# Gradient of w_k by block products after the loop, and the last output pair by block products too

## The chip, the cores and the metric

The kernel runs on one core of one Trainium2 chip. TensorE (PE) multiplies matrices into PSUM; VectorE (DVE) and ScalarE (ACT) do the elementwise work and read PSUM; GpSimd (POOL) and SyncE (SP) issue most of the DMA transfers, each in its own order. The metric is the device time of one execution in microseconds; the lower the better. The time before is the median of three runs, 796.74 us.

## What is computed

The reference is a transformer block, forward and backward, with S = 2048 rows, D = 640 and F = 1728: layernorm, linear attention with 32 heads of 20 columns, output projection, residual, second layernorm, SwiGLU feed-forward (g = silu(x w_gate), u = x w_up, out = (g u) w_down), residual.

```python
x = A_x
h = x + _A_ref(_layernorm(x, axis=-1), A_wqkv, A_wo)
h2 = h + _B_ref(_layernorm(h, axis=-1), B_w_gate, B_w_up, B_w_down)
return h2
```

Outputs are h2 and, for a given grad_out, the gradients of x, w_qkv (640 x 1920: columns of q, k and v), w_o, w_gate, w_up and w_down, all in bfloat16. Two of these matter here. The **gradient of w_k** is xnᵀ · dk, a 640 x 640 result summed over 2048 rows: xn is the normalised input (S x D), dk the gradient at k. The **output** h2 is h1 + m · w_down, where m = g u is S x 1728 and h1 the residual after attention.

## The kernel before, in words

Rows come in ST = 16 tiles of 128 (`P`), columns of D in two halves of 320 (`NCH`), since one PSUM bank takes them singly. PSUM is a pool of four buffers of two banks each (`mm`), handed out in turn. Large SBUF tiles come from pools, also in turn: `big` (five buffers, tag B), `strips` (four buffers, tag S), and two work pools (`wk`). A new tile of a pool waits until the last reader of the buffer's former tile is done.

The work around the change is the end of the kernel. **The dxn loop** (t from 0 to ST + LAG - 1 = 18): for t < 16 it forms dk of row tile t (`ps_dk`, ten matmuls of 320 columns; VectorE finishes dk), and SP issues a DMA transpose of it into `ring`. Three turns later (u = t - LAG) it forms dxn of row tile u (`ps_dxn`, 30 matmuls: dq, pk and dk, all transposed in `ring`, against weights). `load_pqT` brings the transposes of pk and dq three turns ahead; dq itself lies in two strips buffers, `dq[0]` and `dq[1]`, and the transpose of its row tile 15 is the last reader of `dq[1]`. `ln_bwd` then takes dxn through the layernorm's backward: ACT `lb_dy` (L144), DVE reduction (L146) and `lb_k` (L149), ACT `lb_a` (L150), two DVE additions (L151, L152), and a POOL store.

**The gradient of w_k** (`dwqk(1, i)`, i = 0 to 4, L986) takes per 128 rows of the result 2 x 16 matmuls of 320 columns. Tiles 0 to 2 stand in turns 16, 17 and 18 of the loop, ahead of dxn of row tiles 13, 14 and 15; tiles 3 and 4 are filled in behind it in pieces (`dwqk_steps`), between the gradients of w_o (`dwo`) and the first output pair.

**The output stage**: `load_mT` brings m transposed, one DMA transpose per row tile on SP's queue (L1028), four row tiles to a strips buffer; the first five are issued in the loop, the rest later. Row tiles go in pairs. A pair is a 2 x 2 block product with seven products of blocks instead of eight (Winograd's form of Strassen's method): `osum` makes the sums S1 to S4 of the blocks of m on VectorE, T1 to T5 are sums of blocks of w_down made once, and `step_a` to `step_f` (`c22` among them) are the products and the combinations; each pair has 50 matmuls of 320 columns. `NP` = 7 pairs go so; the loop over p runs the first half of pair p between the second half of pair p - 1. Row tiles 14 and 15 are multiplied directly (`tail`, L1266), the last in column chunks of 320, 192 and 128 (`CH15`). `dwv` (gradient of w_v) and `dwo` are filled in once per turn from `small_q`.

Within `tc.manual_schedule` the named engines run in the order in which the code is written; the others are ordered by a scheduler. SP and the DVE are so named around all of this, PE and ACT in the output stage.

Of the kernel before, what the change touches and what calls it, by code (L numbers as in the profile page):

```python
# [15 lines left out]
P = 128  # L16
# [4 lines left out]
def kernel(  # L21
# [901 lines left out]
    with tc.manual_schedule(engines={EngineType.SP, EngineType.DVE}):  # L923
# [71 lines left out]
        def dwqk(which, i, between=None):  # L995
            for n, _ in enumerate(dwqk_steps(which, i)):
                if between and n == 1:
                    between()
# [26 lines left out]
        def load_mT(t):  # L1025
            if t % 4 == 0:
                mTs[t // 4] = strips.tile([P, 4, FT, P], BF16, name="mT", tag="S")
            nc.sync.dma_start_transpose(out=mTs[t // 4][:, t % 4], in_=scr_m[t * P:(t + 1) * P, :])  # L1028

        for t in range(ST + LAG):  # L1030
            if t in (2, 3):
                dwqk(0, t + 1)
# [26 lines left out]
            u = t - LAG  # L1059
            if u < 0:  # L1060
                continue
            if t >= ST:
                dwqk(1, t - ST)
            pkT, dqT, dkT = ring[:, 4 + u % 3], ring[:, 7 + u % 3], ring[:, u % 4]
            ps = mm("ps_dxn")
            for ci, (n0, n1) in enumerate(NCH):
# [3 lines left out]
                                         start=(k == 0 and i == 0), stop=(k == 2 and i == DT - 1))  # L1070
            if u + 3 < ST:
                load_pqT(u + 3)
            if ST - MTA <= u:
                load_mT(u - ST + MTA)
            dx = wk("dx")
            ln_bwd(ps, xn_r[:, u, :], rstd1[:, u:u + 1], dh1[:, u, :], dx[:], 0)
            nc.gpsimd.dma_start(out=o1_v[:, u, :], in_=dx[:])
# [20 lines left out]
            h1rs[t] = wk("h1r", pool=t % 2)  # L1098
            nc.gpsimd.dma_start(out=h1rs[t][:], in_=scr_h1_v[:, t, :])

        NP = ST // 2 - 1
        HK = 6
        ot = big.tile([P, ST * D], BF16, name="ot", tag="B")
        os = big.tile([P, ST * D], BF16, name="os", tag="B")
        B11, B12 = wd[:, 0:HK, 0:320], wd[:, 0:HK, 320:D]
        B21, B22 = wd[:, HK:2 * HK, 0:320], wd[:, HK:2 * HK, 320:D]
        T1, T2, T3, T4 = (ot[:, i * HK * 320:(i + 1) * HK * 320].rearrange("p (k n) -> p k n", k=HK) for i in range(4))
        T5 = ot[:, 4 * HK * 320:4 * HK * 320 + D].rearrange("p (k n) -> p k n", k=2)
        f1 = ot[:, 4 * HK * 320 + D:].bitcast(FP32)
        s1h, u3h = f1[:, 0:320], f1[:, 320:D]  # L1110
        f2 = os[:, 8 * HK * P:].bitcast(FP32)
        u2h = [f2[:, 0:320], f2[:, 320:D]]

        def os_v(p, i):
            o = (4 * (p % 2) + i) * HK * P
# [2 lines left out]
        def mblk(p, r, k):  # L1118
            t = 2 * p + r
            return mTs[t // 4][:, t % 4, k * HK:(k + 1) * HK, :]  # L1120

        def tt(out, in0, in1, op=ALU.subtract):
            nc.vector.tensor_tensor(out=out, in0=in0, in1=in1, op=op)

        def osum(p, i):

# [5 lines left out]

        pa = {}
        pcc = None
        small_q = [(dwo, HG - 1)] + [(dwv, i) for i in range(DT)]

        def prod(out, lhs, rhs, start, stop):
            for k in range(HK):
                nc.tensor.matmul(out, lhsT=lhs[:, k, :], rhs=rhs[:, k, :], start=(start and k == 0),  # L1139
                                 stop=(stop and k == HK - 1), skip_group_check=not start)  # L1140

        def left(out, t, rhs, h, which=(0, 1)):

# [10 lines left out]
        def bank(p):  # L1154
            return pa[p][:, 0, :320], pa[p][:, 1, :320], pcc[:, p % 2, :320]

        def step_a(p):
            pa[p] = mm("ps_oa")
            A, Dk, _ = bank(p)
            prod(A, mblk(p, 0, 0), B11, True, True)  # L1160
            prod(Dk, mblk(p, 0, 1), B21, True, True)
            left(Dk, 2 * p, BL[0], 0)
            tt(s1h, A, h1v(2 * p, 0), ALU.add)
            tt(h1v(2 * p, 0), Dk, s1h, ALU.add)

        def step_b(p):
            prod(bank(p)[2], os_v(p, 0), T1, True, True)

        def step_c(p):
            A = bank(p)[0]  # L1170
            prod(A, os_v(p, 1), T2, False, True)
            tt(u2h[p % 2], A, h1v(2 * p, 1), ALU.add)

        def step_d(p):
            A = bank(p)[0]
            left(A, 2 * p + 1, BL[1], 1, which=(1, 0))
            prod(A, os_v(p, 2), T3, False, True)
            tt(u3h, A, h1v(2 * p + 1, 1), ALU.add)

        def c22(p):  # L1180
# [4 lines left out]

        def step_e(p):
            A = bank(p)[0]
            prod(A, mblk(p, 1, 1), T4, False, True)
            left(A, 2 * p + 1, T5, 0)
            tt(h1v(2 * p + 1, 0), A, h1v(2 * p + 1, 0), ALU.add)  # L1190
            o_store(2 * p + 1)
            pa.pop(p)

        def step_f(p):
            C = pcc[:, p % 2, :320]
            left(C, 2 * p, BL[1], 1, which=(1, 0))
            prod(C, os_v(p, 3), B22, False, True)
            tt(h1v(2 * p, 1), C, u2h[p % 2], ALU.add)
            o_store(2 * p)

        CH15 = [(0, 320), (320, 512), (512, 640)]

        with tc.manual_schedule(engines={EngineType.PE, EngineType.Activation}):
            for t in range(4):
                load_h1(t)
            for t in (5, 6):
                load_mT(t)
            for j in range(2):
                tr_cols(Y[:, j, :], scr_Yt, OH[j])
            tt(T1, B12, B11)  # L1210
            osum(0, 0)
            tt(T2, B22, T1)
            osum(0, 1)
            tt(T3, B22, B12)
            osum(0, 2)
            fill = dwqk_steps(1, 3)
            for j in range(4):
                next(fill)
                dwo(j)
            fill = dwqk_steps(1, 4)  # L1220
            next(fill)
            dwo(4)
            pcc = mm("ps_oc")

            for p in range(NP):
                v = p - 1
                load_h1(2 * p + 4) if 2 * p + 4 < ST else None
                load_h1(2 * p + 5) if 2 * p + 5 < ST else None
                for t in (2 * p + 7, 2 * p + 8):
                    if t < ST:  # L1230
                        load_mT(t)
                for j in range(2 * p + 2, min(2 * p + 4, HG)):
                    tr_cols(Y[:, j, :], scr_Yt, OH[j])
                step_a(p)
                if v < 0:
                    tt(T4, B21, T2)
                    next(fill)
                    step_b(p)
                    step_c(p)
                    osum(p + 1, 0)  # L1240
                    osum(p + 1, 1)
                    next(fill)
                    next(fill)
                    tt(T5, BL[0], BL[1])
                    for k, i in ((0, 3), (1, 2), (1, 3)):
                        osum(p + k, i)
                    continue
                step_d(v)
                step_b(p)
                c22(v)  # L1250
                osum(p + 1, 0)
                step_c(p)
                step_e(v)
                osum(p + 1, 2)
                step_f(v)
                osum(p + 1, 1)
                osum(p + 1, 3)
                if p != 2:
                    f, i = small_q.pop(0)
                    f(i)  # L1260

            pso = {}

            def tail(u, n0, n1, out):
                for j in range(FT - 1):
                    nc.tensor.matmul(out, lhsT=mTs[u // 4][:, u % 4, j, :], rhs=wd[:, j, n0:n1],  # L1266
                                     start=(u == ST - 2 and j == 0), stop=(u == ST - 1 and j == FT - 2))

            v = NP - 1
            p14 = mm("ps_o")  # L1270
            tail(ST - 2, 0, 320, p14[:, 0, :320])
            for f, i in small_q:
                f(i)
            step_d(v)
            tail(ST - 2, 320, D, p14[:, 1, :320])
            c22(v)
            step_e(v)
            step_f(v)
            p15 = [mm("ps_o") for _ in range(2)]
            o15 = [p15[ci % 2][:, ci // 2, :n1 - n0] for ci, (n0, n1) in enumerate(CH15)]  # L1280
            parts = [(ST - 2, n0, n1, p14[:, ci, :320]) for ci, (n0, n1) in enumerate(NCH)]
            parts += [(ST - 1, n0, n1, o15[ci]) for ci, (n0, n1) in enumerate(CH15)]
            for n, (u, n0, n1, out) in enumerate(parts):
                r = slice(64 * (n % 2), 64 * (n % 2) + 64)
                nc.tensor.matmul(out, lhsT=mTs[u // 4][r, u % 4, FT - 1, :], rhs=wd[r, FT - 1, n0:n1],
                                 start=(u == ST - 1), stop=(u == ST - 2))
            tt(half(h1rs[ST - 2][:]), row(p14), half(h1rs[ST - 2][:]), ALU.add)
            o_store(ST - 2)
            h1r = h1rs.pop(ST - 1)
            for ci, (n0, n1) in enumerate(CH15):  # L1290
                tail(ST - 1, n0, n1, o15[ci])
                tt(h1r[:, n0:n1], o15[ci], h1r[:, n0:n1], ALU.add)
                (nc.sync, nc.scalar, nc.sync)[ci].dma_start(out=o0_v[:, ST - 1, n0:n1], in_=h1r[:, n0:n1])


# [28 lines left out]
```

## Time and profile before

| what | before |
|---|---|
| median of the three runs | 796.74 us (796.57 to 804.1) |
| profiled execution: its own time | 796.25 us |
| its span, first to last instruction | 794.5 us |
| PE busy | 790.2 us, 99% of the span |
| DVE busy | 566.9 us, 71% |
| ACT busy | 288.1 us, 36% |
| POOL busy | 172.7 us, 22% |
| DMA moved | 160.11 MB, mean 202 GB/s |
| granted PE clock | 1.000 (mean of the span) |

The profile's own time is 1.75 us above the span, and 0.49 us below the median. Times of single instructions below count from the start of the span. A matmul is pipelined: its busy time, 299 ns for 320 columns, overlaps the next one's, so the rate is read from starts of runs of matmuls: 30 of them in 4.08 us. "Busy" on PE is therefore no measure of distance from the peak.

### The profile page before, as it was taken

The page shows a single profiled execution, that of the slowest core. Times are in us where ns is not written, and L with a number is a line of the kernel's source. Part 1 is how long each engine was busy: PE and PEld are TensorE (multiplying, and loading weights), DVE is VectorE, ACT ScalarE, POOL GpSimd, SP SyncE. Part 2 cuts the span into 40 slices and gives each one's busy share as a digit, 9 for nine tenths or more (in the row PEclk, how much of TensorE's full clock was granted, in tenths as well). Part 3 has the DMA queues.
Part 4 walks back from the last instruction along what each step waited for, and adds up shares of the span by engine and source line. Part 5 has one row for each costly group of instructions (what it writes and reads, how often), then busy time and mean ns, then how long its engine had stood idle before and what let it go on. Part 6 is the DMA issues. An engine that isn't in the chain of part 4 may idle for free.

```text
span 794.5 us, 13629 instructions
## 1 busy us (share of the span) xinstructions
PE 790.2 (99%) x5315; PEld 506.5 (64%) x5315; DVE 566.9 (71%) x1015; ACT 288.1 (36%) x414; POOL 172.7 (22%) x305
## 2 busy tenths in 40 slices
PE   9999999999999999999999999999999999999998
PEld 7776566555555555555666777777777777777665
DVE  7989988894497648845975259998897366635773
ACT  6962532760283045402831123223313133324010
POOL 4600047411201110012042102111221121113230
PEclk9999999999999999999999999999999999999999
DMA  9799999999679877892798657976598959999992
GB/s 259 161 241 305 198 225 254 257 264 234 176 160 236 211 175 191 217 246 68 147 216 217 247 152 193 211 197 168 127 238 177 177 135 155 189 223 261 208 259 83
DMA packets 286705, 160.11 MB, mean 202 GB/s; under 512 B 241564, under 2 KB 275485, under 8 KB 286640
## 3 DMA queue, kind: packets, MB, share of 16 engines
q1 hardware_dynamic: 268912, 99.56, 61.7%
q0 software_dynamic: 14832, 54.36, 22.4%
q10 hardware_dynamic: 2896, 5.33, 2.0%
q8 instruction: 41, 0.67, 0.4%
q14 instruction: 24, 0.20, 0.1%
HBM read 47.68 MB, written 53.66 MB: 128 GB/s over the span
## 4 chain that ended last, share of the span: by engine, by line
PE 97%; DMA 1%; DVE 1%; POOL 0%; issue 0%; SPq 0%; DVEq 0%
PE ps_dhn L108 15%; PE ps_dw L806 10%; PE ps_dxn L1069 8%; PE pu L736 7%; PE ps_wa L646 7%; PE pg L731 7%; PE ps_dwqk L986 5%; PE ps_dm L417 5%; PE ps_kq L305 4%; PE ps_oa L1139 4%; PE ps_wc L646 3%; PE ps_gt L861 3%; PE ps_dp L108 3%; PE ps_dk L108 3%; PE ps_y L508 3%; PE ps_a L571 3%
## 5 line engine op out<-in xcount | busy, mean ns | idle before, releaser
L108 PE MATMUL ps_dhn<-wgT,cols 128*128 128x320 bf16 x864 | 119.5, 299 | 0.0
L108 PEld LDWEIGHTS <-cols 128*128 128x128 bf16 x864 | 84.5, 98 | 32.9
L146 DVE CUSTOM_DVE_ANT_0 lb_a<-lb_dy,hn 128x640 bf16<-128x640 bf16 x32 | 26.4, 825 | 59.0 <-ACT lb_dy L144 59.0
L736 PE MATMUL pu<-wgu,hnT 128*128 128x448 bf16 (+1 forms) x320 | 63.6, 346 | 0.0
L731 PE MATMUL pg<-wgu,hnT 128*128 128x448 bf16 (+1 forms) x320 | 63.6, 346 | 0.0
L806 PE MATMUL ps_dw<-m_s,dh 128*128 128x448 bf16 (+1 forms) x320 | 60.4, 346 | 0.0
L1069 PEld LDWEIGHTS <-ring 128*128 128x128 bf16 x480 | 47.0, 98 | 18.2
L1069 PE MATMUL ps_dxn<-wqkvT,ring 128*128 128x320 bf16 x320 | 51.3, 299 | 0.0
L736 PEld LDWEIGHTS <-hnT 128*128 128x128 bf16 x320 | 31.3, 98 | 27.1
L806 PEld LDWEIGHTS <-dh 128*128 128x128 bf16 x320 | 31.3, 98 | 27.1
L731 PEld LDWEIGHTS <-hnT 128*128 128x128 bf16 x320 | 31.3, 98 | 27.0
L417 PEld LDWEIGHTS <-dh2T 128*128 128x128 bf16 x320 | 31.0, 98 | 25.1
L417 PE MATMUL ps_dm<-wdT,dh2T 128*128 128x448 bf16 (+1 forms) x240 | 46.5, 344 | 0.0
L144 ACT ACTIVATE lb_dy<-ps_dhn,rstd 128x640 bf16<-128x640 f32 x16 | 12.7, 794 | 91.5 <-PE ps_dhn L108 91.5
L305 PE MATMUL ps_kq<-wqk,xnT 128*128 128x320 bf16 x320 | 44.9, 299 | 0.3 <-DMA wqk<-in_A_wqkv_dram 0.2
L752 ACT ACTIVATE dd<-pg 128x896 bf16<-128x896 f32 (+1 forms) x32 | 28.5, 891 | 40.4 <-PE pg L731 38.0
L642 DVE TENSOR_TENSOR dd<-dd 128x3584 bf16<-128x3584 bf16 (+1 forms) x12 | 23.1, 1954 | 22.8 <-PE ps_wa L646 15.6
L305 PEld LDWEIGHTS <-xnT 128*128 128x128 bf16 x320 | 30.9, 98 | 12.7 <-issue 0.5
L646 PEld LDWEIGHTS <-S 128*128 128x128 bf16 x256 | 25.1, 98 | 21.7
L772 POOL DMA_DIRECT2D scr_m<-m_s x16 | 12.1, 758 | 122.6 <-DVE m_s L764 122.6
L986 PEld LDWEIGHTS <-hn 128*128 128x128 bf16 x320 | 31.0, 98 | 12.0
L150 ACT ACTIVATE lb_a<-hn,lb_k 128x640 bf16<-128x640 bf16 x32 | 29.5, 920 | 21.8 <-DVE lb_k L149 18.8
(210 smaller groups left out, 1527.1 us busy)
## 6 DMA issues: line engine op xcount, KB each, us to landing
scr_dT<-stg SPq DMA_DIRECT2D x48, 224.0 KB, 2.6
cols<-scr_dT POOLq DMA_DIRECT2D x6, 1728.0 KB, 8.4
scr_m<-m_s POOLq DMA_DIRECT2D x12, 448.0 KB, 4.6
cols<-scr_dT ACTq DMA_DIRECT2D x2, 1728.0 KB, 10.5
scr_dT<-stg SPq DMA_DIRECT2D x16, 192.0 KB, 2.3
scr_pq<-pqa SPq DMA_DIRECT2D x4, 640.0 KB, 4.6
scr_xnT<-xnT SPq DMA_DIRECT2D x4, 640.0 KB, 5.3
scr_pk<-pk SPq DMA_DIRECT2D x4, 640.0 KB, 4.6
```

Source lines behind the costliest of these rows:

```text
L108: nc.tensor.matmul(ps[:, ci, :320], lhsT=lhs(k), rhs=rhs(k, *NCH[ci]), start=(start and k == 0), stop=(stop and k == n - 1))
L150: nc.scalar.activation(out=a[:], in_=xhat, func=ACT.Identity, scale=k[:, 1:2], bias=k[:, 0:1])
L305: nc.tensor.matmul(ps[:, ci, :320], lhsT=xnT[:, t, k, :], rhs=wqk[:, k, w0 + n0:w0 + n1], start=(k == 0), stop=(k == DT - 1))
L417: nc.tensor.matmul(ps[:, c, :w], lhsT=dh2T[:, kt, (t + c) * P:(t + c + 1) * P], rhs=wdT[:, kt, o:o + w], start=(kt == 0), stop=(kt == DT - 1))
L646: nc.tensor.matmul(out, lhsT=lhs[:, t, :], rhs=rhs[:, t, :], start=(first and t == 0), stop=(t == 7), skip_group_check=not first)
L731: nc.tensor.matmul(pg[:, c, :w], lhsT=hnT[:, kt, (t + c) * P:(t + c + 1) * P], rhs=wg[:, kt, 0:w], start=(kt == 0), stop=(kt == DT - 1))
L736: nc.tensor.matmul(pu[:, c, :w], lhsT=hnT[:, kt, (t + c) * P:(t + c + 1) * P], rhs=wg[:, kt, w:2 * w], start=(kt == 0), stop=(kt == DT - 1))
L752: sig = nc.scalar.activation(out=dg, in_=pg[:, :, :w], func=ACT.Sigmoid)
L806: nc.tensor.matmul(ps[:, c, :w], lhsT=lhs(t), rhs=rhs(t), start=(t == 0), stop=(t == ST - 1))
L986: nc.tensor.matmul(ps[:, ci, :320], lhsT=xn_r[:, t, i * P:(i + 1) * P], rhs=dq[t // 8][:, t % 8, n0:n1] if which == 0 else dk[:, t, n0:n1] ...
L1069: nc.tensor.matmul(ps[:, ci, :320], lhsT=lhs[:, i, :], rhs=rhs[:, i, n0:n1], start=(k == 0 and i == 0), stop=(k == 2 and i == DT - 1))
L1139: nc.tensor.matmul(out, lhsT=lhs[:, k, :], rhs=rhs[:, k, :], start=(start and k == 0), stop=(stop and k == HK - 1), skip_group_check=not s ...
```

## The change

The gradient of w_k leaves the loop. Its result has five row tiles of 128. Tiles 0 to 3 are now taken as two pairs of tiles, with the sum over 2048 rows cut in two halves (`k` = 0, 1, eight row tiles each) and the columns in two halves: again a 2 x 2 block product by seven products, here of 8 matmuls for each of the two tiles (`u`) of a block: 112 matmuls. VectorE makes the sums: `ksum` S1 and S3 of blocks of xn (128 x 1024 each) in turns 16 to 18 of the loop, S2 and S4 later; X1 to X4 (128 x 2560 each) of blocks of dk after the loop. Tile 4 is multiplied directly at the very end, in column chunks of 320, 192 and 128 (`k_tile`), among the last steps of the last output pair. The eighth output pair goes by block products like the others, so `tail` is gone. The sums need room: `sk`, a new strips tile (also for two kept partial results), is allocated in turn 16; `ot` (T1, T2, T4, T5) moves to a strips buffer; T3 is written over B12; `dt` (X1 to X4) takes a big buffer. The m transposes start one turn later.

In the built program, sk has the buffer that dq[1] had, and its first writer, `ksum(1, 0)`, waits for the DMA transposes of dq row tiles 13, 14 and 15. On VectorE it stands right ahead of `ln_bwd` of row tile 13, and X1 right behind `ln_bwd` of row tile 15.

```diff
+        def sk_v(i, u):
+            o = (2 * (i // 2) + u) * 8 * P
+            return sk[:, o:o + 8 * P].rearrange("p (k c) -> p k c", c=P)
+        def ksum(i, u):
+            if i == 1:
+                tt(sk_v(1, u), xb(1, 0, u), xb(1, 1, u), ALU.add)
+            else:
+                tt(sk_v(3, u), xb(0, 0, u), xb(1, 0, u))
...
-            if t >= ST:
-                dwqk(1, t - ST)
+            if t == ST:
+                sk = strips.tile([P, 7 * 8 * P], BF16, name="sk", tag="S")
+                ksum(1, 0)
+            if t == ST + 1:
+                ksum(3, 0)
+                ksum(3, 1)
+            if t == ST + 2:
+                ksum(1, 1)
...
-            if ST - MTA <= u:
-                load_mT(u - ST + MTA)
+            if ST - 4 <= u:
+                load_mT(u - ST + 4)
...
-        NP = ST // 2 - 1
+        NP = ST // 2
-        ot = big.tile([P, ST * D], BF16, name="ot", tag="B")
         os = big.tile([P, ST * D], BF16, name="os", tag="B")
+        dt = big.tile([P, 4, 8, 320], BF16, name="dt", tag="B")
+        ot = strips.tile([P, 3 * HK * 320 + D], BF16, name="ot", tag="S")
...
+            pk_a = [mm("ps_ka") for _ in U]
+            for u in U:
+                prod(pk_a[u][:, 0, :320], xb(0, 0, u), K11, True, 8)
+            tt(X1, K12, K11)
+            for u in U:
+                prod(pk_a[u][:, 1, :320], xb(0, 1, u), K21, True, 8)
+            for u in U:
+                tt(S2[u], S1[u], xb(0, 0, u))
+            tt(X2, K22, X1)
+            ev = wk("dwk", pool=1)
+            for u in U:
+                s1 = wk("s1", pool=u).bitcast(FP32)
+                nc.scalar.copy(out=s1, in_=pk_a[u][:, 0, :320])
+                tt(ev[:, 320 * u:320 * u + 320], pk_a[u][:, 1, :320], s1, ALU.add)
+            k_store(ev, 0, 0)
+            dwo(0)
+            pk_c = mm("ps_kc")
+            for u in U:
+                prod(pk_c[:, u, :320], S1[u], X1, True, 8)
+            tt(X3, K22, K12)
+            tt(X4, K21, X2)
+            dwo(1)
+            for u in U:
+                prod(pk_a[u][:, 0, :320], S2[u], X2, False, 8)
+                nc.scalar.copy(out=kept[:, 0, u, :], in_=pk_a[u][:, 0, :320])
             tt(T1, B12, B11)
             osum(0, 0)
+            dwo(2)
+            for u in U:
+                prod(pk_a[u][:, 0, :320], S3[u], X3, False, 8)
+                nc.scalar.copy(out=kept[:, 1, u, :], in_=pk_a[u][:, 0, :320])
+            for u in U:
+                tt(S1[u], xb(0, 1, u), S2[u])
+            dwo(3)
...
+            for u in U:
+                prod(pk_a[u][:, 0, :320], xb(1, 1, u), X4, False, 8)
+                nc.scalar.copy(out=ev[:, 320 * u:320 * u + 320], in_=pk_a[u][:, 0, :320])
+            k_store(ev, 1, 0)
...
                 if v < 0:
                     tt(T4, B21, T2)
-                    next(fill)
+                    tt(T3, B22, B12)
+                    osum(p, 2)
+                    k_last(0)
+                    pcc = mm("ps_oc")
                     step_b(p)
+                    k_last(1)
+                    ev = wk("dwk", pool=0)
+                    tt(half(ev[:]), pk_c[:, :, :320], kept[:, 0], ALU.add)
+                    k_store(ev, 0, 1)
                     step_c(p)
-                    osum(p + 1, 0)
-                    osum(p + 1, 1)
-                    next(fill)
-                    next(fill)
                     tt(T5, BL[0], BL[1])
-                    for k, i in ((0, 3), (1, 2), (1, 3)):
-                        osum(p + k, i)
+                    osum(p, 3)
+                    for i in range(4):
+                        osum(p + 1, i)
                     continue
...
-            p14 = mm("ps_o")
-            tail(ST - 2, 0, 320, p14[:, 0, :320])
-            for f, i in small_q:
-                f(i)
+            k_tile(*last[0], nc.sync)
             step_d(v)
-            tail(ST - 2, 320, D, p14[:, 1, :320])
+            k_tile(*last[1], nc.sync)
             c22(v)
             step_e(v)
             step_f(v)
...
-            for ci, (n0, n1) in enumerate(CH15):
-                tail(ST - 1, n0, n1, o15[ci])
-                tt(h1r[:, n0:n1], o15[ci], h1r[:, n0:n1], ALU.add)
-                (nc.sync, nc.scalar, nc.sync)[ci].dma_start(out=o0_v[:, ST - 1, n0:n1], in_=h1r[:, n0:n1])
+            k_tile(mm("ps_kl")[:, 0, :128], 512, D, nc.scalar)
```

## The prediction

> **What bounds the kernel now.** First the busy table and the chain that ended last, on the page: the chain says which engine's work adds up to the span, which a busy share can't.
>
> ```profile
> PE 790.2 (99%) x5315; PEld 506.5 (64%) x5315; DVE 566.9 (71%) x1015; ACT 288.1 (36%) x414; POOL 172.7 (22%) x305
> ...
> PE 97%; DMA 1%; DVE 1%; POOL 0%; issue 0%; SPq 0%; DVEq 0%
> ```
>
> 97% of the chain is matmuls: a matmul removed is a gain as long as nothing else comes late. So the second view is the timeline of the end of the loop, PE first.
>
> ```profile
> 697.85 4.51 PE L986 MATMUL ps_dwqk<-dk,hn 128*128 128x320 bf16 x32
> 702.20 0.84 PE L1069 MATMUL ps_dxn<-wqkvT,ring 128*128 128x320 bf16 x5
> ...
> 706.27 4.51 PE L986 MATMUL ps_dwqk<-dk,hn 128*128 128x320 bf16 x32
> ...
> 714.70 4.51 PE L986 MATMUL ps_dwqk<-dk,hn 128*128 128x320 bf16 x32
> ```
>
> The starts are what counts: 32 matmuls from 697.85 to 702.20, 4.35 us, or 0.136 each. These three runs stand between dxn of row tiles 12, 13, 14 and 15, and they are what the change takes away there. What do they cover? The same stretch on VectorE:
>
> ```profile
> 699.03 0.83 DVE L146 CUSTOM_DVE_ANT_0 lb_a<-lb_dy,hn 128x640 bf16<-128x640 bf16 x1 [0.89 <-ACT lb_dy L144]
> ...
> 701.58 0.49 DVE L152 TENSOR_TENSOR dx<-lb_a,dh 128x640 bf16<-128x640 bf16 x1
> 707.39 0.82 DVE L146 CUSTOM_DVE_ANT_0 lb_a<-lb_dy,hn 128x640 bf16<-128x640 bf16 x1 [5.32 <-ACT lb_dy L144]
> ```
>
> One `ln_bwd` holds VectorE from 699.03 to 702.07, 3.0 us with its wait for ACT in the middle, and starts 1.2 us behind the end of its dxn. Then VectorE is idle for 5.3 us per turn, only because PE does `dwqk` meanwhile. Last, SP's queue and what a transpose of dq takes to land (the trace's DMA issues from 690 on):
>
> ```profile
> 697.45 1.29 SPq L973 DMA_TRANSPOSE ring<-dq  x1
> 698.84 1.50 SPq L1028 DMA_TRANSPOSE mT<-scr_m  x1
> 700.44 1.29 SPq L1044 DMA_TRANSPOSE ring<-dk  x1
> 701.83 1.23 SPq L972 DMA_TRANSPOSE ring<-scr_pk  x1
> 703.10 1.27 SPq L973 DMA_TRANSPOSE ring<-dq  x1
> ```
> ```profile
> ring<-dq SPq DMA_TRANSPOSE x3, 3.9
> ```
>
> SP issues without a pause, so row tile 15's dq is issued at 703.10 and lands about 3.9 us later. Nobody minds before; the change makes VectorE wait for it.
>
> **What is removed on PE.** Four tiles of w_k go from 4 x 32 to 112 matmuls (16 fewer), the last pair from 56 to 50 (the direct form has 14 per row tile and half, in units of 320 columns): 6 fewer. Tile 4 of w_k has the same columns as before. 22 x 0.136 = **3.0 us less PE work**. This is all the change can win; PE had no gap to close (its longest wait, 1.1 us, is at the very start).
>
> **What comes late instead: X1.** I walk both engines from 697.85.
> PE: dxn 13 to 15, 3 x 4.08, ends at 710.1; the first products need no sums (32 matmuls, 4.35) and one `dwo` takes 0.27: 714.7. Now it needs X1.
> VectorE: with mT(0) gone from its place (698.84 to 700.44), dq 15 is issued at 701.5 and lands at 705.4. `ksum(1, 0)` waits for that, and `ln_bwd` of row tile 13 stands behind it on VectorE; ACT in turn can't take `lb_a` before. A sum of 128x1024 is priced by the row of the same operation elsewhere in the kernel, one of 128x2560 by another:
>
> ```profile
> L642 DVE TENSOR_TENSOR S<-hn 128x1024 bf16<-128x1024 bf16 x16 | 9.9, 682 | 0.0
> ...
> L464 DVE TENSOR_TENSOR tzs<-pqa,zb 128x2560 bf16<-128x2560 bf16 x4 | 5.9, 1486 | 0.0
> ```
>
> Back to back, each starts about 0.08 us before the busy time of the one ahead ends (1.15 us rows start 1.07 apart). So: 705.4 + 0.6 = 706.0; `ln_bwd` 13 to 709.0; two sums, 710.2; `ln_bwd` 14 to 713.2; one sum, 713.8; `ln_bwd` 15 to 716.8; X1 ready at 718.25. **PE waits 718.25 - 714.7 = 3.55 us.** VectorE is the bound of this stretch: 4 sums and 3 times 3.0 us, without a break after the late start.
>
> **Two smaller waits behind it.** PE takes the X1 products (2.17) and a `dwo` (0.27): 720.7. The next products need X2, and the accumulation goes on in the PSUM tile that VectorE reads for the first stored block: two S2 sums (1.2), X2 (1.4), one addition (0.5) put it at 721.3: **0.6 us**. From there three runs of 16 matmuls (6.5), two `dwo` (0.55) and `step_a(0)` (1.9) bring PE to 730.25 with X3, X4, T1 and T2 ready before they are asked for. Then `k_last`, `step_b`, `k_last`, `step_c`, `step_a(1)`, `step_d(0)`, `step_b(1)`, 56 matmuls, 7.6 us: 737.9. VectorE has from 730.3 on: two additions (1.0), T4 and T3 (2.15), a sum (0.5), the 640-wide addition (0.8), one more (0.45), T5 (0.4), five sums (2.35), two additions (0.95), 738.9 in all, and `step_c(1)` waits for the last: **1.1 us**. Before, T3 and one sum were made ahead of `step_a(0)`, and 16 matmuls of `dwqk` covered the rest (VectorE was idle for 0.82 us at 738.3).
>
> **What costs nothing, and under which cover.** `ring`: dxn 14 now starts at 701.9 instead of 710.6; its dq, issued at 697.45, lands at 701.35, a margin of 0.6; dxn 15 at 706.0 against 705.4, also 0.6. If these fail, PE waits, but VectorE's chain is the later one, so the wait is mostly not added. The copy of the first partial result (ACT) waits for the store of dx 14: 713.2, 0.55 to issue, 3.3 to 5.4 to land, 719.2 at worst against 720.7. ACT's copies of 128x320 aren't in the trace; below 0.69 (the 640 row), 0.45 by the 532 ns of 448 columns; no queue behind them is late. POOL issues ten half-size stores for five, 0.54 each, 2.7 us of an engine that is 22% busy; h1r of pair 1, loaded behind the store of dx 15 (716.8), lands some 5.3 us after its issue and is asked for at 737. SP: mT(8) waits for sk to come free (735) and holds two transposes of Y and mT(9) behind it; before it was issued at 738, so no loss. T3, written in place with a stride of 640, I take like T1, 1.15; twice that would add up to 1.1 at `step_c(1)`. The last store: ACT copy and DMA instead of VectorE addition (0.29) and DMA, 128 columns both; within 0.2 either way.
>
> **Sum.** -3.0 + 3.55 + 0.6 + 1.1 = +2.25, say +2.3 on the profiled execution's 796.25 us (span 794.5 + 1.75): 798.55. That execution is 0.49 below the median of the runs, which is 796.74; so **799.0 us**. Landing bounds the big term: transposes into `ring` landed in 2.6 to 6.4 us in this stretch, so it is 2.2 to 6.1.
>
> [...]
>
> **Rivals.** *A: the sums are hidden, faster.* If the dq transposes have landed when VectorE is free (702.1), `ln_bwd` 13 to 15 start 1.2 behind their dxn, X1 is ready at 715.7, and the wait is 1.0; with the two small waits the sum is -0.3, and -3.0 if none of them is there. Taken as -1.5: 795.2 us. For it: a turn of dxn takes PE 4.08 us, and VectorE needs 3.0 and 0.6 to 1.2 in it, so it can nearly keep up. Against: SP's row at 703.10; the issue would have to come 3 us earlier than SP's pause-free row of transposes lets it.
> *B: the m transposes are late, slower.* Place: the sums of m for the next pair. The windows of the trace show DMA engines full here:
>
> ```profile
> 723.00:737.00 14.00, 14.00 (x104) 9.87 (x102) 10.67 (x19) 5.64 (x9) 6.50 (x12) 1.00 1.18 238
> ```
>
> (the columns at the end: granted clock, DMA share, GB/s). mT(7) landed at 744.8, mT(11) at 759.7, mT(15) at 773.6; the last was first used at 787.5. Now the sums of pair 3 want mT(7) at 746.5, and those of pair 7 want mT(15) at 775.4: 1.7 and 1.8 us of slack. mT(0) is issued 4 us later than before, ahead of wd as before, and mT(1) behind wd. Beyond a lateness of 1.8 us each microsecond is added. A train 4 us late costs 2.2, 801.2 us; one late by 4 and by mT(2)'s long issue of 7.1 (711.15 to 718.25) on top costs about 9, past 1%.
> That PE's order is other than written is no rival: in the built program it has 20 instructions fewer (48 in column chunks for 32 among them), as above.
>
> **Chances.** Forecast 0.55 (797 to 801), A 0.2, B 0.2, the rest for a wait I have not seen, 0.05. The range reaches into A and B: 795.0 to 803.0. 1% is 8 us, about what a measurement of this kernel can tell from no change; only all of B's worst end is past it. Faster 0.02, same 0.92, slower 0.06.
>
> **What will show it.** The first 128x1024 sum into sk starting at 705 or later, with VectorE idle before it for a DMA; `ps_kc` waiting 3 to 4 us on VectorE's dt; short waits at `ps_ka` and, in the second pair, `ps_oa`; PE's matmuls 20 fewer; no wait of VectorE on mT. Wrong if sk's first sum starts at 702 (A), if sums `os<-mT` wait for DMA (B), or if the granted clock falls below 1.00 behind the gap.

## The result, and the profile after

The changed kernel takes **801.83 us** (median of 22 executions, 799.3 to 805.19) against 796.56 for the kernel before (median of 22 beside them): a ratio of 1.0059, 95% interval [1.0044, 1.0073]. It is slower by about 5 us, inside 1%, inside the range of 795 to 803, 2.8 us above the forecast of 799.0, and above the 797 to 801 that the forecast gave itself. The profiled execution took 801.46 us (span 799.7), 5.2 more than that of before; the forecast was 2.25 more.

The page of the changed kernel, busy table and chain:

```profile
PE 789.5 (99%) x5295; PEld 504.1 (63%) x5295; DVE 582.5 (73%) x1038; ACT 288.7 (36%) x420; POOL 174.0 (22%) x308
...
PE 88%; DVE 5%; DMA 5%; ACT 0%; POOL 0%; SPq 0%; issue 0%; DVEq 0%
```

20 matmuls fewer, as said; but the chain that ended last was 97% PE and is 88%: 10% of it now runs through VectorE and DMA. The waits, PE's and then VectorE's (total us, times, longest), say where:

```profile
PE ps_kc L1162 <- DVE dt L1033: 4.0, 1, 4.0
PE ps_oa L1162 <- DVE h1r L1033: 0.8, 1, 0.8
...
DVE sk L1033 <- DMA ring<-dq: 4.3, 1, 4.3
```

The cause and the effect, in the timelines of SP, VectorE and PE (start, us, instruction, idle time before it):

```profile
702.48 1.27 SPq L973 DMA_TRANSPOSE ring<-dq  x1
```
```profile
701.70 0.49 DVE L152 TENSOR_TENSOR dx<-lb_a,dh 128x640 bf16<-128x640 bf16 x1
706.53 0.69 DVE L1033 TENSOR_TENSOR sk<-hn 128x1024 bf16<-128x1024 bf16 x1 [4.33 <-DMA ring<-dq]
707.14 0.82 DVE L146 CUSTOM_DVE_ANT_0 lb_a<-lb_dy,hn 128x640 bf16<-128x640 bf16 x1
...
717.83 1.49 DVE L1033 TENSOR_TENSOR dt<-dk 128x2560 bf16<-128x2560 bf16 x1
```
```profile
714.92 0.43 PE L1110 MATMUL ps_dwo<-mats 128*128 128x320 bf16 x2
719.37 3.18 PE L1162 MATMUL ps_kc<-dt,sk 128*128 128x320 bf16 x16 [4.01 <-DVE dt L1033]
722.35 0.74 PE L1110 MATMUL ps_dwo<-mats 128*128 128x320 bf16 x2
722.88 2.96 PE L1162 MATMUL ps_ka<-dt,os 128*128 128x320 bf16 x16
```

VectorE stands from 702.2 to 706.5 until the transpose of dq 15, issued at 702.48, has landed; `ln_bwd` 13 starts behind it at 707.14, X1 is made at 717.83, and PE, free at 715.2, starts the X1 products at 719.37. Then look at the starts: these 16 matmuls take 2.98 us, to 722.35, where 16 such take 2.17 elsewhere. The table of windows has the reason (columns: window, its length, busy time of PE, PEld, VectorE, ScalarE and POOL, then the granted clock, the DMA share and GB/s):

```profile
715.20:719.37 4.17, 0.16 (x2) 0.00 (x0) 3.08 (x7) 1.24 (x2) 1.56 (x3) 1.00 1.21 272
719.37:722.35 2.98, 2.98 (x17) 1.90 (x17) 2.98 (x5) 1.03 (x3) 0.00 (x0) 0.73 1.28 297
722.35:725.68 3.33, 3.33 (x20) 2.13 (x19) 3.33 (x4) 1.12 (x2) 2.17 (x4) 0.73 1.16 253
725.68:728.39 2.71, 2.71 (x22) 1.96 (x20) 2.58 (x4) 1.51 (x4) 1.08 (x2) 1.00 1.20 320
```

Behind the gap the granted clock is 0.73 in two stretches, 6.31 us together, and 0.27 of that, 1.7 us, is what the fall costs. From `step_a(2)` on PE runs without a gap to the end.

### The profile page after: what moved, and what is told of

It is laid out like the page before. It is cut to its first block, busy times and chain, and to the rows that moved or that the text cites. A ratio compares the mean times of both kernels' runs of the same rounds, so it can differ in the third digit from the quotient of the medians.

```text
span 799.7 us, 13627 instructions
## 1 busy us (share of the span) xinstructions
PE 789.5 (99%) x5295; PEld 504.1 (63%) x5295; DVE 582.5 (73%) x1038; ACT 288.7 (36%) x420; POOL 174.0 (22%) x308
## 4 chain that ended last, share of the span: by engine, by line
PE 88%; DVE 5%; DMA 5%; ACT 0%; POOL 0%; SPq 0%; issue 0%; DVEq 0%
PE ps_dhn L108 15%; PE ps_dw L806 8%; PE ps_dxn L1095 7%; PE ps_wa L646 7%; PE pg L731 6%; PE pu L736 6%; PE ps_dm L417 5%; PE ps_oa L1162 4%; PE ps_kq L305 4%; PE ps_wc L646 3%; PE ps_dwqk L986 3%; PE ps_gt L861 3%; PE ps_dk L108 3%; PE ps_dp L108 3%; PE ps_y L508 3%; PE ps_a L571 3%
## 5 line engine op out<-in xcount | busy, mean ns | idle before, releaser
L885 POOL DMA_DIRECT2D pqr<-scr_pq x16 | 8.8, 548 | 112.6 <-PE ps_dp L108 112.6
```

## The experiments

All rows were measured beside the kernel before. "Loop to end" is the profiled execution's time from the first dxn matmul to the end of the span; what lies ahead of it is the same code in all, and moves by up to 1.5 us from execution to execution (3.5 in e8's). The profiled execution is one of those counted in the median, and not always a typical one: in e14 and e15 it is the fastest of twelve, in e8 the slowest of ten. The loop to the end is 165.9 for the kernel before and 171.0 for the changed one.

| kernel | median us | ratio [95%] | loop to end |
|---|---|---|---|
| changed kernel | 801.83 | 1.0059 [1.0044, 1.0073] | 171.0 |
| order (e1) | 802.38 | 1.0064 [1.0044, 1.0084] | 168.2 |
| warm (e3) | 801.21 | 1.0074 [1.0055, 1.0093] | 169.3 |
| pair alone (e4) | 798.34 | 1.0021 [1.0000, 1.0043] | 166.7 |
| five edits (e5) | 803.20 | 1.0081 [1.0068, 1.0095] | 170.7 |
| buffers (e8) | 801.84 | 1.0060 [1.0038, 1.0082] | 173.3 |
| order + buffers (e9) | 805.88 | 1.0105 [1.0087, 1.0122] | 173.5 |
| all edits (e10) | 802.62 | 1.0066 [1.0045, 1.0087] | 172.4 |
| w_k alone (e11) | 796.73 | 0.9992 [0.9971, 1.0013] | 166.1 |
| split tile (e12) | 797.78 | 1.0000 [0.9980, 1.0020] | 168.2 |
| all edits, dwv later (e13) | 798.55 | 1.0014 [0.9994, 1.0035] | 169.3 |
| split, dwv later (e14) | 796.38 | 0.9986 [0.9957, 1.0015] | 164.7 |
| split, dwv apart (e15) | 794.69 | 0.9987 [0.9967, 1.0007] | 163.8 |

**Order: is it `ln_bwd` 13 behind the wait?**

```diff
             if t == ST:
                 sk = strips.tile([P, 7 * 8 * P], BF16, name="sk", tag="S")
+            if t == ST + 1:
                 ksum(1, 0)
-            if t == ST + 1:
                 ksum(3, 0)
```

> The changed kernel with one line moved: ksum(1, 0) is issued one turn of the loop later, behind ln_bwd of row tile 13. It still needs the same DMA (dq of row tile 15, landing at about 706.5 us of the span), but ln_bwd 13 no longer stands behind it on VectorE. My theory (the late X1 is ln_bwd 13 held up by that wait): ln_bwd 13 starts some 4 us earlier, X1 is ready at about 716.4, PE waits about 1.2 us for it instead of 4.2, the short wait for X2 comes back (0.6), the granted clock stays at 1.00 behind it: 3.0 from the wait and 1.7 from the clock, less 0.6, about 4.0 us less, 797.8 us. The rival (VectorE has simply more to do in this stretch than PE's time gives it, whatever the order): X1 stays near 718, time 801.8 us.

The waits on PE in the profiled execution, and ScalarE's timeline:

```profile
PE ps_dwo L1110 <- ACT dwo L1111: 1.9, 1, 1.9
...
PE ps_kc L1162 <- DVE dt L1033: 0.9, 1, 0.9
PE ps_oa L1162 <- DVE h1r L1033: 0.8, 1, 0.8
```
```profile
719.69 0.75 ACT L1256 COPY s<-ps_ka 128x320 f32<-128x320 f32 x2 [5.36 <-DMA out_dram<-dx]
720.33 0.71 ACT L1111 CAST dwo<-ps_dwo 128x640 bf16<-128x640 f32 x1
```

The mechanism holds: with the order changed the wait for X1 is 0.9 us, the clock stays at 1.00, and that execution took 799.29 us. But a second wait stands behind the first. ScalarE's copy of the first partial result takes a buffer that the store of dx 14 still reads; the store was issued at 712.05 and landed 7.6 us later. PE needs the next copy, of dwo(0), to have its PSUM tile back. And over six executions nothing is won: four took 802 to 804 us, each with a mean clock of 0.998, and what held these four isn't traced. The forecast of 797.8 fails.

**Warm: does the clock cost by itself?**

```diff
             dwo(0)
             pk_c = mm("ps_kc")
+            for _ in range(3):
+                prod(pk_c[:, 1, :320], xb(0, 0, 0), K11, True, 8)
```

> The changed kernel with 24 more matmuls of 128x320 between dwo(0) and the first products with X1, 3.3 us of PE work in the gap; their results are written into a PSUM bank that is overwritten afterwards and are used by nothing. PE still can't start the X1 products before X1 is ready. Theory (the 4.0 us of idle time drops the granted clock to half for a stretch behind it, and that is a cost by itself): PE idles for about 0.9 us, the clock is 1.00 in all stages, the 16 matmuls behind the gap take 2.2 us instead of 3.0; X2, which the slow clock hid, costs its 0.6: 1.7 less 0.6, about 1.1 us faster than the changed kernel, 800.7 us, with 3.3 us MORE work on PE. Rival (what the clock record shows doesn't set the time): the same as the changed kernel, 801.8 us, or slower by what the added matmuls cost behind X1.

```profile
716.21 3.42 PE L1162 MATMUL ps_kc<-dk,hn 128*128 128x320 bf16 x24
719.47 2.34 PE L1162 MATMUL ps_kc<-dt,sk 128*128 128x320 bf16 x16
721.64 0.43 PE L1110 MATMUL ps_dwo<-mats 128*128 128x320 bf16 x2
```

In the profiled execution the 24 matmuls fill the gap, the X1 products take 2.17 us at a clock of 1.00, and from the loop to the end it is 1.8 us shorter with 3.3 us more work. The medians (801.21 and 801.83) and the ratios don't tell the two apart, so the clock's price is shown by the stages, not by the time. The changed kernel's own executions fit: the two with a mean clock of 1.00 took 799.3 and 800.3 us, the four with 0.995 took 802.6 to 805.2; but these six have no trace, so how long their gaps were is not shown.

**The last pair alone, in the kernel before.**

```diff
-        NP = ST // 2 - 1
+        NP = ST // 2
...
-                if p != 2:
+                if p not in (2, NP - 1):
```

and the end is `step_d`, the last `dwv`, `c22`, `step_e`, `step_f` in place of the direct form.

> The kernel before with one part of the change alone: the last output pair by block products as the other seven (50 matmuls of 320 columns in place of 56), the direct tail and its 640-wide pieces gone; the gradient of w_k stays as it was in the kernel before. Theory (this part is worth its 6 matmuls, 0.8 us, less a longer end behind the last product): 796.4 us, within 0.6 of the kernel before. Rival (the pair is the costly part of the change, by its sums of m or by the end of the chain): 2 us or more over the kernel before, 798.6 us or above.

The loop to the end is 0.8 longer, where 0.2 shorter was forecast; the median is 1.8 higher. Six matmuls are saved, but PE waits 0.3 for VectorE, and the end is 1.1 longer: behind the last matmul come an addition of 320 columns (0.49) and a store of 160 KB (1.8 to land), where it was 128 columns (0.29) and 32 KB (1.4). So this part costs something by itself.

**Five edits at once.** The order of e1, T3 and `osum(0, 2)` ahead of `step_a(0)`, the first chunk of the fifth tile into the gap, the last store on SP:

```diff
             dwo(0)
+            k_tile(wk("dwl", pool=0), mm("ps_kl")[:, 0, :320], 0, 320, nc.gpsimd)
             pk_c = mm("ps_kc")
...
-            k_tile(mm("ps_kl")[:, 0, :128], 512, D, nc.scalar)
+            k_tile(ev, mm("ps_kl")[:, 0, :128], 512, D, nc.sync)
```

> The order of the first experiment (ksum(1, 0) behind ln_bwd 13) and three more edits on what the trace of the changed kernel shows as waits: the first 320 columns of the last tile of w_k's gradient (16 matmuls, 2.2 us, needing no sums) are done in PE's gap ahead of the X1 products instead of at the very end; T3 and the sum osum(0, 2) are made ahead of step_a(0); the last store goes on SP's queue instead of ScalarE's. Theory: of 797.8 us the rests of the X1 and X2 waits go (1.8), the wait in step_c(1) goes (about 1.0), and the end is shorter by 0.6: 794.4 to 795.4 us, faster than both kernels. Rival (the block products can't win because VectorE is short of time throughout the stretch): the waits come back elsewhere, 797 us or above.

It was slower than the changed kernel, not faster than both as forecast, for the wait that e1 had just shown:

```profile
PE ps_kc L1162 <- ACT dwo L1111: 4.1, 1, 4.1
```
```profile
720.86 0.75 ACT L1264 COPY s<-ps_ka 128x320 f32<-128x320 f32 x2 [6.44 <-DMA out_dram<-dx]
```

X1 was ready at 716.9, yet the products began at 722.26: the store of dx 14 took 9.1 us to land. One edit did what it should. The last store (issues: KB each, us to landing), first the changed kernel's, then this one's:

```profile
out_dram<-dwk ACTq DMA_DIRECT2D x1, 32.0 KB, 2.2
```
```profile
out_dram<-dwk SPq DMA_DIRECT2D x1, 32.0 KB, 1.4
```

**Buffers, and both.** The copies are freed from the store; e8 has this alone, e9 with the order of e1.

```diff
-                s1 = wk("s1", pool=u).bitcast(FP32)
+                s1 = u2h[u]
...
-            ev = wk("dwo", pool=j % 2)
+            ev = wk("dwo", pool=(j // 2 + 1) % 2)
```

> The changed kernel with other buffers for two of ScalarE's copies behind the gap: the first partial results (s1) go into a free part of os, and the output of dwo(0) into the other pool, so that neither waits for the store of dx of row tile 14 to land (719.0 us in the profiled execution of the changed kernel; in the first experiment's, where X1 was ready at 716.8, the same store landed at 719.7 and held PE by 1.9 us). The order on VectorE is as in the changed kernel, so X1 still comes at about 719.4. Theory (the store is a second cause of about the same lateness, and what spreads the times): the wait for X1 and the clock's fall stay, time about 801, but with less spread above it than the changed kernel's 799.3 to 805.2. Rival (the store plays no part): 801.8 us with the same spread.

> Both edits together: ksum(1, 0) behind ln_bwd 13, and the two copies free of the store of dx 14. Theory (two causes of the gap, either enough by itself): PE waits 0.9 us for X1 and about 0.5 for X2, none on ScalarE's copies; the granted clock is 1.00 in every execution; 797.2 to 798.5 us. Rival (the store is not what holds the first experiment's executions at 802): 801.5 us or more.

Alone the buffers change nothing, nor is the spread smaller (798.25 to 807.1), so the wait of these two copies for the store is not what spreads the changed kernel's times. That no store does is not shown: in e8's profiled execution VectorE itself waited for one, in `ln_bwd` 15 right ahead of X1, since the buffer of dx 13 was still being stored, and the copies, now in `os`, waited for `ln_bwd` 15.

```profile
723.13 0.49 DVE L152 TENSOR_TENSOR dx<-lb_a,dh 128x640 bf16<-128x640 bf16 x1 [2.25 <-DMA out_dram<-dx]
```

(That execution also had a wait of 2.4 us far ahead of the loop and one of 2.2 for a dq; its stage time isn't used.) Both edits together were the worst kernel of all, 805.88 us where 797.2 to 798.5 was forecast, with a clock under 1.00 in all six executions; this is what taught most. PE's timeline:

```profile
716.91 2.35 PE L1162 MATMUL ps_kc<-dt,sk 128*128 128x320 bf16 x16 [0.90 <-ACT dwo L1111]
719.10 0.43 PE L1110 MATMUL ps_dwo<-mats 128*128 128x320 bf16 x2
719.92 2.33 PE L1162 MATMUL ps_ka<-dt,os 128*128 128x320 bf16 x16 [0.38 <-DVE dwk L1033]
...
755.32 0.38 PE L127 MATMUL ps_dwv<-stg,mats 128*128 128x120 bf16 x5
760.04 0.23 PE L127 MATMUL ps_dwv<-stg,mats 128*128 128x120 bf16 x1 [4.34 <-DMA mats<-scr_Yt]
```

The gap at X1 is closed: 0.9, and 0.4 for X2. But dwv(0), which PE takes at 758.9 in the changed kernel and at 758.0 before, is now reached at 755.3, and the last transpose of Y (an operand of `dwv`, brought on SP's queue too) is not there. SP's queue, from the first of these transposes on:

```profile
709.80 28.68 SPq L1028 DMA_TRANSPOSE mT<-scr_m  x6
738.52 2.58 SPq L938 DMA_TRANSPOSE mats<-scr_Yt  x2
```

Six transposes of m took 28.7 us to issue, with two of Y behind them; in the changed kernel they took 17.6. The last two of Y, first in the changed kernel, then here:

```profile
745.46 2.59 SPq L938 DMA_TRANSPOSE mats<-scr_Yt  x2
```
```profile
753.55 3.49 SPq L938 DMA_TRANSPOSE mats<-scr_Yt  x2
```

The later one of each two landed 6.4 and 4.6 us after its issue, at 753.2 and at 760.4. So in these traces PE pays 4 us at X1 with the gap, and 4 us at the transposes without it. But two things moved: PE came 3.5 us earlier and Y 7.2 us later. With Y at 753.2, PE at 755.3 would not have waited. Why the queue ran later is not settled: the issues are longer one by one, with the same transfers (over the 16 of m a median of 2.85 us and a longest of 9.28, against 2.28 and 6.69 in the changed kernel), and the DMA engines' share from 698 to 770 is 1.08 in the changed kernel and 1.16 in the one before, in e9 1.22 from 716 to 720 and 1.19 from 755 to 762. That closing the gap makes the queue late is not shown either: e11, without a gap, met Y in time.

**All edits**, that is e5 with the buffers of e8 and the chunk's `dwl` in pool 1; and the same with dwv one turn later:

> Both edits, and the three of the fourth experiment that were lost behind the store: the first 320 columns of w_k's fifth row tile in the gap ahead of the X1 products, T3 and osum(0, 2) ahead of step_a(0), the last store on SP's queue. Theory: of 797.7 us the rests of the waits for X1 and X2 go (1.4, covered by 2.2 us of work that leaves the end), 0.5 to 1.0 of the wait in step_c(1), and 0.6 at the end: 795.0 us, under the kernel before by about 1.5. Rival (the freed time is lost to another transfer): 797 us or more.

```diff
+            def k_mid(i):
+                k_tile(wk("dwl", pool=1), mm("ps_kl")[:, 1, :192], 320, 512, nc.gpsimd)
+
+            small_q = [(dwo, 4), (dwo, 5), (k_mid, 0)] + [(dwv, i) for i in range(DT)]
...
-            k_tile(ev, mm("ps_kl")[:, 1, :192], 320, 512, nc.sync)
+            for f, i in small_q:
+                f(i)
```

> The third experiment of the last series (both edits, fifth tile's first chunk in the gap, T3 early, last store on SP; PE waited 4.7 us at dwv(0) for the transposes of Y, with two windows of half clock) with the dwv one turn later: the 192-column chunk of the fifth tile, which needs no transpose, takes dwv(0)'s place in the third pair, and the last dwv stands at the end in its place. Theory (behind the closed gap the next bound is SP's queue of transposes, which PE reaches 4 us earlier): the wait at dwv(0) goes, with its clock; up to 3 us can come back as waits of the sums for m; 795 to 798.5 us, against 802.6. Rival (that wait is not what holds it): 801 us or more.

e10 had no wait left at X1 or X2, but 4.7 us at dwv(0). Behind that, 12 matmuls of 320 columns take 3.16 us from start to start where 12 such at 748.2 take 1.63, and the granted clock of this execution is 0.995 in the mean: 802.62 where 795.0 was forecast. (One of its twelve executions kept a clock of 1.00; it took 796.3.) With other work put into that turn (e13) this wait went and the time fell by 4.1 us, to 798.55, just above the forecast of 795 to 798.5. PE then waits 2.4 us for a dq in `ring`, and 2.6 in all for VectorE, where the next lateness shows:

```profile
DVE os L1033 <- DMA mT<-scr_m: 7.7, 4, 2.9
```

**w_k's block products alone.** Both edits, T3 in X1's space and early, the whole fifth tile (32 matmuls) ahead of the X1 products, and the direct last pair and end of the kernel before. Then three refinements: half of the tile between dxn 13 and 14, and `osum(1, 2)`, `osum(1, 3)` behind `step_c(1)` (e12); no dwv in the pair p = 3 (e14); the last two dwv apart (e15).

```diff
             if t == ST + 1:
+                tile4(0)
...
+            tile4(1)
             pk_c = mm("ps_kc")
...
-                f, i = small_q.pop(0)
-                f(i)
+                if p != 3:
+                    f, i = small_q.pop(0)
+                    f(i)
```

> Both edits, T3 (in the space of X1) and osum(0, 2) ahead of step_a(0), the whole fifth row tile of w_k's gradient (32 matmuls, 4.4 us, needing no sums) in the gap ahead of the X1 products, and the last output pair by the direct form and with the end of the kernel before. What is left of the change is w_k's block products alone: 16 matmuls fewer than before, 2.2 us. Theory: no wait for X1 or X2 is left, 0.5 us in step_c(1), and the end is that of the kernel before: 796.5 - 2.2 + 0.5 = 794.8 us. Rival (VectorE's sums come too late even so): 796.5 us or above.

> The previous experiment's best form (w_k's block products, the fifth tile ahead of X1, direct last pair) with two more edits. One half of the fifth row tile (16 matmuls, 2.2 us) goes between dxn of row tiles 13 and 14, where the kernel before has dwqk, so that the dq transposes have 2.2 us more (their wait was 1.6 us there); X1 had 3.4 us to spare. And osum(1, 2) and osum(1, 3) are made behind step_c(1), which waited 0.5 us. Theory (these two waits are all that is left of the cost): 796.7 - 1.6 - 0.5 = 794.6 us, under the kernel before by 2. Rival (the end of the kernel is set by the transposes of m and Y, whatever PE does before): 796.5 us.

> The split form (w_k's block products, fifth tile in two halves, direct last pair) with the dwv products one turn later: none in the pair p = 3, two at the end. In the split form's profiled execution all waits were gone but one, 2.5 us at dwv(0) for the transposes of Y, with a window of half clock behind it (1.7 us); half of its executions showed such a window. Theory: these go, 796.9 + 1.7 - 2.5 - 1.7 = 794.4 us, about 2 us under the kernel before, with a granted clock of 1.00 nearly always. Rival (the sums for m, which PE now reaches 2 to 4 us earlier, wait for their transposes instead): 796.5 us or above.

> The last form with its two final dwv products apart (one ahead of step_d, one ahead of c22): back to back, the second waited 0.8 us for ScalarE's copy of the first, the last wait on PE behind the start. Theory: 0.8 less in the profiled execution, a span of about 792.3 us against the kernel before's 794.5, and a ratio near 0.997, its interval under 1. Rival (the freed time is lost to the sums or the stores at the end): as the last form, 0.9986 or above.

e11 is even with the kernel before (0.9992), 1.9 us above its expectation; its largest wait is a transpose into `ring`:

```profile
PE ps_dxn L1095 <- DMA ring<-dq: 1.6, 1, 1.6
```

e12 took that wait away and got nothing for it (797.78, forecast 794.6), since PE, at dwv(0) 2.4 us earlier, met the last transposes of Y: it waited for them until 758.67 and again until 759.12, where in e11 it ran dwv(0) at 758.43 without a wait:

```profile
758.67 0.23 PE L127 MATMUL ps_dwv<-stg,mats 128*128 128x120 bf16 x1 [2.23 <-DMA mats<-scr_Yt]
```

In e14 this is gone too. Its profiled execution took 794.8 us (span 793.1) where 794.4 was forecast, but its median is 796.38, within noise of the kernel before. In e15's profiled execution no wait is left on PE but two at places where the kernel before waits as well:

```profile
PE 787.9 (99%) x5299; PEld 504.6 (64%) x5299; DVE 579.4 (73%) x1031; ACT 288.7 (36%) x419; POOL 175.1 (22%) x310
...
PE 97%; DVE 1%; DMA 1%; POOL 0%; issue 0%; DVEq 0%
```
```profile
PE ps_warm L341 <- DVE ones L244: 1.1, 1, 1.1
PE ps_kq L305 <- DMA xnT<-xn: 0.3, 1, 0.3
```

Its span is 792.2 us against 794.5, and from the loop to the end it is 2.1 us shorter, which is the 16 matmuls of w_k (2.2). Its fastest execution, the profiled one, took 793.95 us, the fastest of the kernel before 796.00. Its median is 1.8 us under the kernel before (794.69 against 796.52). But the ratio, 0.9987 [0.9967, 1.0007], doesn't exclude no gain, where an interval under 1 was forecast: three of its twelve executions took 799 to 802 us. So it is shown in the profile, and only likely in the time, that it beats the kernel before.

## Why the prediction was right and where it was not

*The range* held partly by luck. 801.83 lies outside the 797 to 801 of the forecast itself, and inside the range only because that was widened for B, late transposes of m, which did not happen in the changed kernel.

*The bound and the saving* were right: 20 matmuls fewer, and output pairs at the pace of before. e15's profile shows what the saving of w_k is worth once nothing is late.

*X1* was right in its mechanism: the dq transpose, the wait of `ksum(1, 0)`, `ln_bwd` 13 behind it, X1 last. e1 shows it by the order alone. The size was 3.55 and is 4.2: SP issued dq 15 at 702.48 where I had 701.5, and it landed at 706.5, not 705.4, while PE itself came 0.5 later. That is 0.6.

*The clock* is the failed step. My sum has no term for it, though I named a clock below 1.00 behind the gap as a sign of being wrong. It came: 0.73 over 6.31 us behind a wait of 4.0, which is 1.7 us. The trace of before has a fall as well, at its very end: PE's last matmul ends at 791.67, and from 793.75 on the granted clock is 0.50. The slow products hid the 0.6 at X2 (no wait on PE there, where e9 at a clock of 1.00 has 0.4), so the fall is worth about 1.1.

*"What costs nothing"* failed in three places. `ring`'s margin of 0.6 was not there: 0.4 us late in the changed kernel, 2.4 in e13. The end was to be even within 0.2, and the last store on ScalarE's queue took 2.2 us to land instead of 1.4, with the span's end 0.6 later. And the store of dx 14, at worst at 719.2 by my count, landed at 719.0 in the changed kernel, hidden beside X1, but at 719.6 and 720.8 in e1 and e5: 7.6 and 9.1 us after its issue, where I had 3.3 to 5.4.

*`step_c(1)`* was 1.1 and is 0.8. Together 2.25 + 0.6 + 1.1 + 0.4 + 0.6 - 0.3 = 4.65; measured 5.2; the remaining 0.55 is not assigned.

*The rivals* were posed as alternatives, and that was the deeper error. A's condition (dq in time, or out of VectorE's way) can be had, by e1's order, and by itself brings nothing: the store of dx 14 comes next, and behind it the lateness that B is about. No sum of m waited for a transpose in the changed kernel, but with gap and store out of the way dwv(0) waited for Y (e9, e10) and the sums for m (e9, e10, e13). The slack of 1.7 to 1.8 us that I found for mT rested on the landings of one trace, and these are not fixed: mT(7), at 744.8 in the kernel before, landed at 737.7 in the changed kernel, and in e13 a sum of m waited 2.9 us for its transpose.

## What to carry to other kernels

Late things can stand in series: before you price the removal of a wait, ask which queue PE will reach earlier, and by how much that queue's last transfer is ahead of it. Don't take that margin from one trace: the last transpose of Y landed at 753.2 in the changed kernel, at 759.1 in e12 and at 760.4 in e9. Work without inputs that are late (here the fifth tile) is well placed ahead of the sums (e11, e15), and a product that needs the last transfers of a full DMA queue is worth moving back by a turn (e13: 4.1 us less than e10; e14: e12's wait of 2.2 us gone). Where PE is going to stand idle, look in the traces at hand for the granted clock behind gaps of that length, and put a fall into the sum: here one of 4.0 us cost 1.7 more.

## What was not expected of the hardware

The clock fell after shorter gaps than the 3.55 us that I had expected: in e12 PE was idle for 2.2 us and 0.2 once more, started again at 759.1, and the granted clock was 0.76 from 759.5 on and 0.50 from 761 to 763:

```profile
759.50:761.00 1.50, 1.50 (x11) 0.92 (x10) 0.00 (x0) 0.59 (x1) 0.84 (x2) 0.76 1.08 320
761.00:763.00 2.00, 2.00 (x9) 0.83 (x8) 0.82 (x2) 0.00 (x0) 0.00 (x0) 0.50 1.21 172
763.00:766.00 3.00, 3.00 (x22) 2.02 (x20) 1.84 (x5) 0.00 (x0) 0.00 (x0) 0.88 1.21 312
```

It did not fall after every gap of that length. The idle times of PE, and the granted clock in the windows behind them (us from the span's start):

| gap on PE | idle, us | granted clock behind it |
|---|---|---|
| e9, at X1 | 0.90 | 1.00 (716 to 720) |
| e1, at X1 and at the copy of dwo(0) | 0.9 and 1.9 | 1.00 (715 to 726) |
| e13, at a dq | 2.4 | 1.000, mean of the whole span |
| e12, at dwv(0) | 2.23 and 0.23 | 0.76 (759.5 to 761), 0.50 (761 to 763), 0.88 (763 to 766) |
| e8, at 195 us | 2.40 | 0.77 (194 to 197), 0.75 (197 to 201) |
| changed kernel, at X1 | 4.01 | 0.73 (719.37 to 725.68) |
| e5, at X1 | 4.1 | 0.57 (722 to 726) |
| e9, at dwv(0) | 4.34 | 0.60 (760 to 764) |

In this table a fall stands behind each of the three gaps of 4.0 us and more, and behind two of the three of 2.2 to 2.4. What decided among these is not shown: no experiment moved a gap to try it, and none has a gap near 3.55 us.

And a 160 KB store on POOL's queue took 2.2 (e1) to 9.1 us (e5, e8) to land beside the transposes.
